# Loading a later pair's keys and values further along in the pair that is being worked on

## The chip, the cores and the metric

The kernel runs on one core of one Trainium2 chip. The metric is the device time of one execution in microseconds, as the median of several runs. The profile is that of one execution of its own.

## The reference, cut to what matters

Three layers follow one another on two batches of 768 positions.

```python
# 1: attention for 2 x 8 heads of 64, masked to pairs whose sign patterns under proj agree
mask = q_bucket[:, :, :, None] == k_bucket[:, :, None, :]
scores = np.where(mask, scale * np.matmul(q, k.transpose(0, 1, 3, 2)), -1e9)
attn = softmax(scores)
x = np.matmul(attn, v)            # heads side by side: 2 x 768 x 512
# 2: a mixing over positions of rank 32, then a two-layer perceptron 512 -> 2048 -> 512
u = x + (x.T @ U @ V).T
x = u + np.maximum(u @ w_ch1, 0.0) @ w_ch2
# 3: four gated causal attention experts, two of them kept at each position
```

The change touches only the loads of `q`, `k` and `v` of the first layer.

## The kernel before, in words

**Pairs and tiles.** The first layer works on two heads at a time, which the kernel calls a pair: four pairs for each batch, numbered here 0 to 7 in their order. A pair has 12 tiles of 128 queries each (`a1_head`, two heads of six). For a tile TensorE makes the scores (L606, L611), VectorE moves them to SBUF with their row minimum (L617), ScalarE takes the exponential (L526, or L575) and a float16 copy (L528), GpSimd or VectorE the remainder that the copy lost (L534). A transposing DMA turns the two halves (L628, `PT<-HL`; in batch 0 some of the buffers are parts of tiles called `more_W` and `more_hT`), and TensorE multiplies by the values (L538 to L540). In batch 0 every second tile keeps float32 and is turned on TensorE in place of the DMA (L581, L590); in batch 1 every tile is turned by the DMA. In batch 0 there are five buffers for each of the scores, the halves and the turned halves, in batch 1 three.

**What a pair does for later pairs.** At the start of pair i, `ahead` first calls `a1_prep` for pair i+1: ScalarE, VectorE and GpSimd make float16 halves of its queries (L403, L404) and keys (L408 on ScalarE, L409 and L414 on GpSimd), three transposing DMAs turn them (AQ L407, AK L412, KT L418), copies go to BQ and BK (L419, L421), and `a1_values` scales and splits the values (L454 on GpSimd, L455 on ScalarE, L456 on GpSimd). Six tiles later `signs` makes the sign patterns, and four small DMAs carry them (L446, L447). Then `a1_load` sets up the loads of pair i+2: six DMAs of 192 KB, one for each head of `q`, `k` and `v`. The buffers `qn`, `kn` and `vn` exist once, so a load must wait until the preparation of the pair before has read them. Every result of a load is needed by the preparation of its pair, which stands in the program at the start of pair i+1.

**What sets the order.** All these DMAs, and the loads of the perceptron's weights (L278, 32 units of 512 KB, three quarters of them within batch 0), are issued by SyncE in one queue (SP). `later(n, fn)` holds a step back until `tick()` has been called n times; `tick()` comes once for each tile. A scheduler of the language then lays the instructions out on the engines by their place in the program and by when it believes them ready, so that an engine with nothing due takes a later step early. On the chip each engine runs its own list in order.

**The other work.** The perceptron's weights are prepared on VectorE, ScalarE and GpSimd during batch 0 (`w64_unit`, L189 to L195 and L281 to L283). From the second half of pair 4 on, the perceptron's matmuls (L734, L754) are interleaved with the tiles, and after the first layer with the third.

Of the kernel before, what the change touches and what calls it, by code (L numbers as in the profile page):

```python
# [22 lines left out]
def kernel(  # L23
# [49 lines left out]
    XP = (0, 40)  # L73
    XV = True
    LUV = 4
    PLAG = (0,150)
    VLAG = 150
    PJ = nc.vector
# [266 lines left out]
    def later(n, fn):  # L345
        pending.append([n, fn])
# [10 lines left out]
    def sooner(n, fn):  # L357
        tc.cur_priority -= n
        fn()
        tc.cur_priority += n  # L360
# [7 lines left out]
    def a1_load(b, p, spread=True):  # L368
        h0 = 2 * p
        qn = sp.tile([P, 2 * NT, D], F32, tag="qn", name=f"qn_{b}_{p}")  # L370
        kn = sp.tile([P, 2 * NT, D], F32, tag="kn", name=f"kn_{b}_{p}")
        vn = sp.tile([P, 2 * NT, D], F32, tag="vn", name=f"vn_{b}_{p}")
        jt = [slice(NT * j, NT * (j + 1)) for j in range(2)]
        todo = []
        for j in range(2):
            todo.append((qn[:, jt[j], :], q[b, h0 + j].rearrange("(t p) d -> p t d", t=NT)))
            todo.append((kn[:, jt[j], :], k[b, h0 + j].rearrange("(p t) d -> p t d", t=NT)))
        for j in range(2):
            todo.append((vn[:, jt[j], :], v[b, h0 + j].rearrange("(p t) d -> p t d", t=NT)))
        nats[b, p] = (qn, kn, vn)  # L380
        todo = [lambda d=d, s_=s_: nc.sync.dma_start(d, s_) for d, s_ in todo]
        if spread:
            for i, fn in enumerate(todo):
                later(1 + i, fn)
        return todo

    preps = {}
# [71 lines left out]
    def a1_first(b, p):  # L459
        n = f"{b}_{p}"  # L460
        todo = a1_load(b, p, False)
        qn, kn, vn = nats.pop((b, p))
        QN = sp.tile([P, 2 * NT, P], FH, tag="QN", name=f"QN_{n}")
# [72 lines left out]
    def pv(o, PT, nk, vh, vl):  # L536
        for t in range(nk):
            nc.tensor.matmul(o, PT[:, t, :], vh(t), start=(t == 0), stop=False)  # L538
            nc.tensor.matmul(o, PT[:, t, :], vl(t), start=False, stop=False)  # L539
            nc.tensor.matmul(o, PT[:, nk + t, :], vh(t), start=False, stop=(t == nk - 1))  # L540
# [54 lines left out]
    def a1_head(b, p, j, xn):  # L595
# [7 lines left out]
        for t in range(NT):  # L603
# [17 lines left out]
            if mode[0] == "F":  # L621
# [6 lines left out]
            nc.sync.dma_start_transpose(out=PT, in_=HL.rearrange("p a s -> p (a s)"))  # L628
            sooner(-PLAG[b], lambda: pv(
                po[:, t, :], PT, NT,  # L630
# [59 lines left out]
    def a1_stream():  # L690
        pairs = [(b, p) for b in range(B) for p in range(NP)]
        for i, (b, p) in enumerate(pairs):
            if p == 0:
                if b == 1:
                    more_buffers(False)
            def ahead(i=i):
                if i + 1 < len(pairs):
                    a1_prep(*pairs[i + 1], SIGN_LAG)
                    if i + 2 < len(pairs):
                        a1_load(*pairs[i + 2])  # L700
                    else:
                        later(SIGN_LAG + 1, moe2_weights)

            if i == 0:
                later(2, ahead)
                later(LUV, load_uv)
            else:
                ahead()
            xn = sp.tile([P, NT, P], F32, tag="xn", bufs=XNB, name=f"xn_{b}_{p}")
            for j in range(2):  # L710
                for c in a1_head(b, p, j, xn):
                    tick()
                    yield c
            later(LAGX, lambda b=b, p=p, xn=xn: sooner(XP[p == NP - 1], lambda: x_stage_a(b, p, xn)))
# [362 lines left out]
    for fn in a1_load(0, 1, False):  # L1077
        fn()
# [126 lines left out]
```

## Time and profile before

| what | value |
|---|---|
| median of 3 runs | 636.65 us (636.04 to 637.46) |
| the profiled execution | 635.59 us, its span 633.8 us |
| TensorE matmul busy | 579.1 us (91%) |
| VectorE busy | 422.7 us (67%) |
| ScalarE busy | 348.5 us (55%) |
| GpSimd busy | 232.1 us (37%) |

A busy share is an average over the whole execution. The first layer takes the first 360 us and does not have the same limit all along; the views below cut it into stretches. The page draws the span in 40 slices of 15.8 us. The granted clock of TensorE is given as a share of full speed: 1.00 is 2.4 GHz and 0.50 is 1.2 GHz.

### The profile page before, as it was taken

The page shows a single profiled execution, that of the slowest core. Times are in us where ns is not written, and L with a number is a line of the kernel's source. Part 1 is how long each engine was busy: PE and PEld are TensorE (multiplying, and loading weights), DVE is VectorE, ACT ScalarE, POOL GpSimd, SP SyncE. Part 2 cuts the span into 40 slices and gives each one's busy share as a digit, 9 for nine tenths or more (in the row PEclk, how much of TensorE's full clock was granted, in tenths as well). Part 3 has the DMA queues.
Part 4 walks back from the last instruction along what each step waited for, and adds up shares of the span by engine and source line. Part 5 has one row for each costly group of instructions (what it writes and reads, how often), then busy time and mean ns, then how long its engine had stood idle before and what let it go on. Part 6 is the DMA issues. An engine that isn't in the chain of part 4 may idle for free.

```text
span 633.8 us, 16209 instructions
## 1 busy us (share of the span) xinstructions
PE 579.1 (91%) x6498; PEld 477.0 (75%) x6498; DVE 422.7 (67%) x1029; ACT 348.5 (55%) x744; POOL 232.1 (37%) x218
## 2 busy tenths in 40 slices
PE   5698888978798799989999999999999999998995
PEld 3376866757577589875888898878887888997963
DVE  6989696988877863674876555583784435465295
ACT  4769485775786652673776543462453413344273
POOL 4738777686897662231432101020040000002021
PEclk9679797889889999999999999999999999999998
DMA  8799999999989999597587602242263102016064
GB/s 234 140 218 215 243 211 244 227 228 269 219 182 251 231 178 172 101 200 114 108 130 121 101 20 50 38 84 72 46 114 67 34 15 39 27 35 109 23 107 109
DMA packets 228029, 84.36 MB, mean 133 GB/s; under 512 B 207057, under 2 KB 223473, under 8 KB 227953
## 3 DMA queue, kind: packets, MB, share of 16 engines
q1 hardware_dynamic: 227952, 83.32, 65.4%
q8 instruction: 51, 0.84, 0.6%
q14 instruction: 26, 0.20, 0.1%
HBM read 29.11 MB, written 3.15 MB: 51 GB/s over the span
## 4 chain that ended last, share of the span: by engine, by line
PE 59%; DMA 14%; DVE 7%; POOL 7%; ACT 6%; issue 5%; SPq 1%; POOLq 0%; DVEq 0%; ACTq 0%
PE px L754 18%; PE ph L734 12%; DMA PT<-HL 8%; PE po L590 3%; POOL HL L534 3%; PE pq L805 3%; PE s L908 2%; PE pk L805 2%; PE pz L1040 2%; PE pv L837 2%; ACT HL L528 2%; DVE P L617 2%; ACT P L526 2%; DMA more_hT<-more_W 2%; DMA more_hT<-HL 2%
## 5 line engine op out<-in xcount | busy, mean ns | idle before, releaser
L534 POOL TENSOR_TENSOR HL<-P,HL 128x768 f16<-128x768 f32 (+5 forms) x62 | 88.7, 1432 | 323.2 <-DVE HL L530 148.7
L734 PE MATMUL ph<-U,W 128*128 128x256 f16 (+1 forms) x1344 | 145.1, 258 | 1.7 <-DVE hT L736 1.1
L754 PE MATMUL px<-hT,W 128*128 128x256 f16 (+1 forms) x1344 | 146.1, 258 | 0.1
L734 PEld LDWEIGHTS <-W 128*128 128x128 f16 x1344 | 114.2, 98 | 17.1 <-issue 2.4
L754 PEld LDWEIGHTS <-W 128*128 128x128 f16 x1344 | 115.0, 98 | 14.3 <-issue 2.0
L526 ACT ACTIVATE P<-P,m 128x768 f32<-128x768 f32 (+5 forms) x109 | 88.7, 814 | 56.0 <-DVE P L916 28.7
L617 DVE TENSOR_SCALAR_CACHE_REDUCE P<-sc 128x768 f32<-128x768 f32 x76 | 71.9, 950 | 12.8 <-PE sc L611 8.4
L736 DVE SCALAR_TENSOR_TENSOR hT<-ph,hT 128x256 f16<-128x256 f32 (+1 forms) x112 | 42.6, 382 | 45.6 <-ACT hT L735 44.9
L528 ACT ACTIVATE HL<-P 128x768 f16<-128x768 f32 (+5 forms) x80 | 60.5, 758 | 17.6 <-DMA PT<-HL 14.8
L735 ACT ACTIVATE hT<-ph 128x256 f16<-128x256 f32 (+1 forms) x112 | 38.7, 347 | 51.3 <-PE ph L734 47.8
L538 PEld LDWEIGHTS <-PT 128*128 128x128 f16 x516 | 47.8, 99 | 23.8 <-DMA PT<-HL 20.1
L606 PE MATMUL sc<-AK,AQ 128*128 128x512 f16 x192 | 50.0, 341 | 9.3 <-DVE P L617 6.5
L538 PE MATMUL po<-V,PT 128*128 128x64 f16 x372 | 45.7, 195 | 11.5 <-DMA PT<-HL 10.6
L611 PE MATMUL sc<-BK,BQ 88*128 88x512 f16 x192 | 49.9, 340 | 0.0
L539 PEld LDWEIGHTS <-PT 128*128 128x128 f16 x516 | 47.5, 99 | 1.5 <-issue 0.2
L540 PEld LDWEIGHTS <-PT 128*128 128x128 f16 x516 | 47.4, 99 | 0.4
L540 PE MATMUL po<-V,PT 128*128 128x64 f16 x372 | 45.7, 195 | 0.0
L539 PE MATMUL po<-V,PT 128*128 128x64 f16 x372 | 45.2, 195 | 0.0
L534 DVE TENSOR_TENSOR HL<-P,HL 128x768 f16<-128x768 f32 (+5 forms) x42 | 32.3, 769 | 15.4 <-ACT HL L528 14.8
L916 DVE TENSOR_SCALAR_CACHE_REDUCE P<-s 128x128 f32<-128x128 f32 (+5 forms) x48 | 29.5, 618 | 10.9 <-PE s L913 10.6
L606 PEld LDWEIGHTS <-AQ 128*128 128x128 f16 x192 | 18.0, 105 | 17.8 <-issue 13.2
L611 PEld LDWEIGHTS <-BQ 88*128 88x128 f16 x192 | 19.5, 102 | 13.9 <-issue 2.1
(240 smaller groups left out, 1186.7 us busy)
## 6 DMA issues: line engine op xcount, KB each, us to landing
w<-in_moe_w_ch_dram SPq DMA_DIRECT2D x16, 512.0 KB
wx<-in_moe_w_ch_dram SPq DMA_DIRECT2D x16, 512.0 KB
qn<-in_q_dram SPq DMA_DIRECT2D x16, 192.0 KB
kn<-in_k_dram SPq DMA_DIRECT2D x16, 192.0 KB
vn<-in_v_dram SPq DMA_DIRECT2D x16, 192.0 KB
out_dram<-o SPq DMA_DIRECT2D x12, 256.0 KB
PT<-HL SPq DMA_TRANSPOSE x101
BQ<-AQ SPq DMA_DIRECT2D x7, 192.0 KB
```

Source lines behind the costliest of these rows:

```text
L526: nc.scalar.activation(P32, P32, AF.Exp, bias=m, scale=-1.0, accum_out=ssum)
L528: nc.scalar.activation(HL[:, 0], P32, AF.Copy)
L534: eng.tensor_tensor(HL[:, 1], P32, HL[:, 0], op=ALU.subtract)
L538: nc.tensor.matmul(o, PT[:, t, :], vh(t), start=(t == 0), stop=False)
L539: nc.tensor.matmul(o, PT[:, t, :], vl(t), start=False, stop=False)
L540: nc.tensor.matmul(o, PT[:, nk + t, :], vh(t), start=False, stop=(t == nk - 1))
L606: nc.tensor.matmul(ps[:, c0 : c0 + cn], aq[:, t, :], ak[:, c0 : c0 + cn], start=True, stop=False,)
L611: nc.tensor.matmul(ps[:, c0 : c0 + cn], bq[:, t, :], bk[:, c0 : c0 + cn], start=False, stop=True,)
L617: nc.vector.tensor_scalar(P32, ps[:, 0:S], CLIP, None, op0=ALU.min, op1=ALU.min, accum_out=m)
L734: nc.tensor.matmul(ph, w, u, start=(i == 0), stop=(i == len(ops) - 1))
L736: nc.vector.scalar_tensor_tensor(hT[1][:, ft, :], ph, 0.0, hT[0][:, ft, :], op0=ALU.max, op1=ALU.subtract)
L754: nc.tensor.matmul(po, w, u, start=(i == 0), stop=(i == len(ops) - 1))
```

## The change

The loads of pair i+2, which were issued after tiles 1 to 6 of pair i in the order q0, k0, q1, k1, v0, v1, are issued after tile 1 (q0), tile 3 (q1), tile 5 (k0), tile 6 (k1), tile 8 (v0) and tile 9 (v1). The queries keep their tiles. The first head's keys move by three tiles, the second head's by two, and the values by three. In pair 0 all of this counts from its third tile on, since `ahead` is called there two tiles late. Pairs 0 and 1 are loaded at the start without a delay, before and after.

```diff
+    LOADS = (1,3,5,6,8,9)
...
         if spread:
-            for i, fn in enumerate(todo):
-                later(1 + i, fn)
+            for i, n in zip((0, 2, 1, 3, 4, 5), LOADS):
+                later(n, todo[i])
         return todo
```

## Rows read from the trace of the kernel before

**Rows 1.** The page: the span, and the granted clock in 40 slices.
```profile
span 633.8 us, 16209 instructions
...
PEclk9679797889889999999999999999999999999998
```

**Rows 2.** Stretches: busy us (instructions) of PE, PEld, DVE, ACT, POOL; clock; DMA.
```profile
30.00:212.00 182.00, 155.99 (x1624) 124.59 (x1623) 149.23 (x288) 129.26 (x241) 133.16 (x115) 0.89 1.06 228
220.00:260.00 40.00, 40.00 (x459) 34.98 (x456) 21.73 (x42) 15.02 (x29) 15.45 (x14) 1.00 0.91 167
64.00:66.00 2.00, 0.55 (x3) 0.31 (x3) 2.00 (x4) 1.13 (x3) 1.84 (x3) 1.00 1.05 201
66.00:73.00 7.00, 6.60 (x60) 6.54 (x61) 2.59 (x8) 2.17 (x5) 5.42 (x5) 0.53 1.08 237
```

**Rows 3.** Timeline of SP, in pairs 0 to 2: start, duration, line, DMA.
```profile
21.70 0.35 SPq L381 DMA_DIRECT2D vn<-in_v_dram  x1
...
65.02 0.59 SPq L381 DMA_DIRECT2D kn<-in_k_dram  x1
65.73 1.74 SPq L628 DMA_TRANSPOSE PT<-HL  x1
...
68.81 0.53 SPq L381 DMA_DIRECT2D kn<-in_k_dram  x1
69.52 3.58 SPq L628 DMA_TRANSPOSE more_hT<-HL  x1
...
73.77 0.43 SPq L381 DMA_DIRECT2D vn<-in_v_dram  x1
...
77.97 0.51 SPq L381 DMA_DIRECT2D vn<-in_v_dram  x1
...
82.41 1.47 SPq L628 DMA_TRANSPOSE more_hT<-more_W  x1
...
90.27 3.42 SPq L412 DMA_TRANSPOSE AK<-KN  x1
93.75 1.28 SPq L418 DMA_TRANSPOSE KT<-KL  x1
...
124.77 2.44 SPq L412 DMA_TRANSPOSE AK<-KN  x1
```

**Rows 4.** Timeline of POOL; in brackets its idle time before and what ended it.
```profile
75.33 0.83 POOL L409 TENSOR_SCALAR KN<-KN 128x768 f16<-128x768 f16 x1 [3.74 <-ACT KN L408]
76.12 2.50 POOL L414 TENSOR_TENSOR KL<-kn,KN 128x384 f16<-128x384 f32 x2
...
80.74 1.64 POOL L534 TENSOR_TENSOR more_W<-more_W,more_W 128x768 f16<-128x768 f32 x1 [0.18 <-ACT more_W L528]
85.25 1.65 POOL L534 TENSOR_TENSOR more_W<-P,more_W 128x768 f16<-128x768 f32 x1 [2.87 <-ACT more_W L528]
...
113.27 0.86 POOL L409 TENSOR_SCALAR KN<-KN 128x768 f16<-128x768 f16 x1 [3.79 <-ACT KN L408]
```

**Rows 5.** The chain that ended last, in order of time: start, duration, what.
```profile
82.41 6.45 DMA more_hT<-more_W
...
97.87 4.96 DMA PT<-HL
...
163.22 6.10 DMA more_hT<-HL
...
189.30 4.14 DMA vn<-in_v_dram
```

**Rows 6.** Who waited for whom from 30 to 212: total us, times, longest.
```profile
POOL KN L409 <- ACT KN L408: 11.5, 4, 3.8
...
PE po L538 <- DMA PT<-HL: 6.3, 6, 2.7
...
PE po L538 <- DMA more_hT<-HL: 4.5, 2, 3.0
...
PE po L538 <- DMA more_hT<-more_W: 3.4, 2, 2.6
```

## The prediction

> **What bounds the kernel now.** I begin with the page. Its clock line has low digits from the second slice to the twelfth (16 to 190 us) and full ones from there almost to the end [rows 1]; so I cut near there. In the table of stretches TensorE is busy all 40.00 of 40 us from 220 to 260, at full clock: from there on TensorE's own work sets the pace, and a DMA that moves inside it is covered [rows 2]. From 30 to 212 us no engine is full: of 182 us TensorE has 155.99 busy, VectorE 149.23, GpSimd 133.16 and ScalarE 129.26, at a mean granted clock of 0.89, while the DMA engines show a share of 1.06 and 228 GB/s [rows 2]. This is the stretch of pairs 0 to 4, and it is the only place where the change can be worth anything.
>
> Inside it the pace comes in waves, one for each pair. At the restart of a pair TensorE runs dry (0.55 busy of 2 us from 64 to 66, with VectorE at 2.00 of 2.00), then it has work again, but for the next 7 us the clock is at its lower level (0.53 on average, 0.50 is 1.2 GHz), and now VectorE and ScalarE idle (2.59 and 2.17 of 7) [rows 2]. One such wave costs 7 x (1 - 0.53) = 3.3 us of TensorE. The chain of waits says what the restart waits for: transposed halves that land 5 to 6 us after SP has issued them [rows 5]. All TensorE's waits for such landings from 30 to 212 us are 6.3 + 4.5 + 3.4 = 14.2 us [rows 6]. That is the pot out of which the change could pay.
>
> **What the change does to SP.** In pair 1 the old order had k0 at 65.02 and k1 at 68.81, each right ahead of a transpose (65.73 and 69.52), v0 at 73.77, and v1 at 77.97 behind the four sign DMAs [rows 3]. In the new order k0 takes about v0's place, k1, at tile 6 behind the signs, about v1's place, and v0 and v1 stand ahead of the transposes of tiles 8 and 10. Nothing is added: the four loads cost SP 0.59 + 0.53 + 0.43 + 0.51 = 2.06 us of issue for a pair, before and after. On the DMA engines one load is 192 KB, which at the 237 GB/s of the stretch from 66 to 73 is an estimate of 0.83 us [rows 2].
>
> **Step 1, the transposes after a restart.** Each k load leaves the way of a transpose: at most 0.59 + 0.83 = 1.4 us. From 66 to 73 TensorE is busy 6.60 of 7 us at half clock, so an earlier landing has nothing to shorten there, and I count nothing for pairs 1 to 3. In pair 4 the restart's landing stands in the chain with 6.10 us, against 4.96 where no load stood ahead [rows 5]. The difference, 1.14, is the most that a load taken away may give; I take half, -0.6. Bounds 0 and -1.1.
>
> **Step 2, the transposes late in a pair.** v0 and v1 now precede transposes that had none. The one at 82.41 is on the chain with 6.45 us until it landed [rows 5], so a load ahead of it can count in full: 0.43 + 0.83 = 1.3 us, in three pairs 3.8. But a tile takes some 3 us and v0 has most of that to drain. I take 0.4 for a pair, +1.2. Bounds 0 and +3.8.
>
> **Step 3, the keys' preparation.** GpSimd waits 11.5 us in four pairs for ScalarE's copy of the keys, 3.74 of it at 75.33, and then spends 0.83 + 2.50 = 3.33 us on them [rows 4, 6]. This lies within the wave's idle part, and the next remainder, at 80.74, was released by ScalarE only 0.18 us before it began, so GpSimd's own wait delayed nothing. With the keys 77.97 - 68.81 = 9.2 us later, the work falls to about 84.5. There GpSimd has a hole of 2.87 us ahead of 85.25 [rows 4], which takes nearly all of the 3.33; the overhang is 0.46 us. In return ScalarE, which has to serve the waiting tiles first after a restart, is rid of one copy of about 0.83 us (taken from GpSimd's row on the same 128 x 768 elements). I take half, 0.4 us, for four pairs: -1.6. Bounds -3.3 (all of it) and +1.8 (the overhang in four pairs).
>
> **Step 4, the last value load of pair 6.** It is on the chain itself, at 189.30 with 4.14 us, stuck behind sign DMAs [rows 5]. Three tiles later it is no longer what these tiles meet. The chain will find another way, mostly a transpose's landing, so I take a third, -1.4. Bounds 0 and -4.1.
>
> **The sum** is -0.6 + 1.2 - 1.6 - 1.4 = -2.4 us. Made against the profiled execution it is 635.59 (its span 633.8, and 1.8 around it) - 2.4 = 633.2. The median of the runs is 1.06 above that execution, so the forecast is 634.25, rounded to 634.2: 0.4% faster. A measurement of this kernel can tell about 0.2%, which is 1.3 us.
>
> **The rivals.**
>
> *The keys fall into the full half of a pair.* If the load lands only a few us later than I assume, its 3.33 us of GpSimd come after 85.25, in the part where VectorE and GpSimd have no hole left and the remainders feed the transposes of the next restart. For it: the hole at 82.4 is the only one seen there; late in a wave VectorE is full. Against it: GpSimd is busy only 133.16 of 182 us. It decides when the keys' first GpSimd step begins after 85 in pair 1. At about 0.9 us for a pair, between the overhang of 0.46 and the full 3.33, four pairs give +3.6: 640.3 us. Slower.
>
> *The keys come too late for their own transposes.* AK and KT stand in SP's queue ahead of the next pair's first transposes, and SP waits at them with everything behind it. In pair 1 GpSimd was done with AK's input at 76.2, and SP got to AK at 90.27: 14 us of slack, 5 after the move. In pair 2 it was 114.13 against 124.77 [rows 3, 4]: 10.6 us of slack, 1.4 after the move of 9.2. The time is bounded from below by nothing, and from above by a wait of the 9.2 us itself in a pair; I put 1 us in two pairs, +2.0: 638.6 us. The Trainium skill, in "DMA: Bandwidth & Descriptors", section "Rules for kernel authors", asks to issue a DMA early and to wait for it late; the change does the reverse, and by that rule it could only lose. The rows agree so far as slack shrinks from 10.6 to 1.4 us, and do not show it used up.
>
> *It is hidden either way.* The queries, which are the first thing needed, keep their tiles, the later loads may be covered by their slack, and what one transpose wins another loses: 636.6 us. To this belongs that the change may do less than it says: the scheduler sent a value load at 21.70, well ahead of the queries of its pair, since nothing else was due [rows 3], and may send the later loads early too. Against that, in pair 1 the order of SP is that of the program.
>
> **How the numbers follow.** The pot is small and no step dominates, and each shift also shifts what the scheduler packs around it; so the chances lie close. My forecast has 0.42, "hidden" 0.25, the full half of a pair 0.20, the late keys 0.13. That gives faster 0.42, same 0.25, slower 0.33. The forecast's own range is 630.0 to 635.4: the low end is the sum, one half-clock wave less (-3.3) and a part of the free bounds of steps 3 and 4. The range over all cases needs the slower rivals, both well over 0.1, so it runs from 630.0 to 641.0, which leaves about 1 in 10 on each side outside.
>
> **What the profile after would show.** SP's list in pair 1 should have one load between each two of its transposes, k1 behind the four sign DMAs, and v1 ahead of the last transpose but none of these loads within the first 5 us after the restart except q0. GpSimd's wait for the keys should shrink from 11.5 us, and its keys' steps should stand some 9 us later. The chain should no longer hold a value load. Step 2 is right if landings late in a pair grow by less than 1 us. The forecast is wrong if the table of stretches shows a new low clock in the middle of a pair, if GpSimd is fuller and VectorE emptier before the restarts, if SP waits at AK or KT for GpSimd, or if TensorE becomes full from 30 us at a later time than now. Since the stretch after 220 is TensorE's alone, whatever is won must show as an earlier start of that full stretch.

## The result and the profile after

The changed kernel takes 641.49 us (median of four runs, 639.4 to 645.47) against 636.35 for the kernel before (four runs, 628.08 to 637.46; three of them are those shown ahead of the prediction): ratio 1.0115, 95% interval 1.0068 to 1.0162, so slower. Here and below the ratio is estimated over the single runs, without runs of a kernel more than 1.5% above its fastest, and is not the quotient of the two medians, which is 1.0081 here. The forecast was 634.2 us with a range of 630.0 to 641.0; the sign was wrong and the time lies just above the range. The profiled execution took 642.95 us, its span is 7.4 us longer than before.

All line numbers past the new one are higher by 2 in the changed kernel: L381 is now L383, L628 L630, L538 L540, L409 L411.

The page of the changed kernel, span and granted clock:

```profile
span 641.2 us, 16217 instructions
...
PEclk9778887998787989999999999999999999999998
```

Against [rows 1], the lower digits reach to the fifteenth slice; from the sixteenth on the two lines are alike. The table of stretches of the changed kernel (columns as in [rows 2]):

```profile
30.00:212.00 182.00, 156.12 (x1538) 122.79 (x1538) 146.00 (x281) 123.86 (x228) 129.66 (x114) 0.84 1.04 221
220.00:260.00 40.00, 38.12 (x413) 32.90 (x410) 19.68 (x36) 15.46 (x29) 13.39 (x12) 0.96 0.82 162
...
76.00:84.00 8.00, 7.68 (x59) 5.28 (x60) 6.71 (x14) 4.92 (x8) 5.51 (x6) 0.57 1.00 261
...
193.00:200.00 7.00, 6.08 (x53) 4.33 (x53) 6.26 (x13) 4.51 (x8) 3.52 (x4) 0.52 1.00 223
```

From 30 to 212 us TensorE is as busy as before (156.12 for 155.99) at a lower clock (0.84 for 0.89), so it gets less done. A new low clock stands in the middle of pair 1 (0.57 from 76 to 84) and late in pair 4 (0.52 from 193 to 200), which the prediction had named as a sign against it. From 220 to 260 TensorE is no longer full (38.12 of 40 us for 40.00), so the stretch that TensorE paces by itself begins later.

Roughly where the time is lost shows in VectorE's closing step of each head (`xn`, two in each pair). Its timeline before, for the sixth to the tenth head and the last:

```profile
133.31 0.55 DVE L639 TENSOR_TENSOR xn<-po,r 128x384 f32<-128x384 f32 x1
150.65 0.56 DVE L639 TENSOR_TENSOR xn<-po,r 128x384 f32<-128x384 f32 x1 [0.16 <-PE po L590]
173.15 0.56 DVE L639 TENSOR_TENSOR xn<-po,r 128x384 f32<-128x384 f32 x1 [3.09 <-PE po L590]
190.98 0.55 DVE L639 TENSOR_TENSOR xn<-po,r 128x384 f32<-128x384 f32 x1
217.34 0.55 DVE L639 TENSOR_TENSOR xn<-po,r 128x384 f32<-128x384 f32 x1
...
363.34 0.55 DVE L639 TENSOR_TENSOR xn<-po,r 128x384 f32<-128x384 f32 x1
```

and the same heads in the changed kernel:

```profile
133.83 0.56 DVE L641 TENSOR_TENSOR xn<-po,r 128x384 f32<-128x384 f32 x1 [0.54 <-PE po L592]
158.02 0.55 DVE L641 TENSOR_TENSOR xn<-po,r 128x384 f32<-128x384 f32 x1
179.06 0.56 DVE L641 TENSOR_TENSOR xn<-po,r 128x384 f32<-128x384 f32 x1 [2.79 <-PE po L592]
202.80 0.56 DVE L641 TENSOR_TENSOR xn<-po,r 128x384 f32<-128x384 f32 x1 [0.39 <-PE po L542]
224.18 0.55 DVE L641 TENSOR_TENSOR xn<-po,r 128x384 f32<-128x384 f32 x1
...
371.35 0.55 DVE L641 TENSOR_TENSOR xn<-po,r 128x384 f32<-128x384 f32 x1
```

At the end of pair 2 the kernels are level (+0.5 us). The changed one is 7.4 behind halfway through pair 3 and 5.9 after it, 11.8 halfway through pair 4 and 6.8 after it, 8.0 at the end of the layer. Pair 1's new low clock thus cost nothing that lasted. By these rows most of the lag stands after pair 3, and pair 4 adds 0.9 to it. They are a rough measure: the place of `xn` in VectorE's list can move, and in pair 4 other matmuls are interleaved.

What pair 3 lost begins at its restart, where TensorE waits for a transpose. Before, in SP's and TensorE's timelines:

```profile
133.25 2.19 SPq L628 DMA_TRANSPOSE more_hT<-HL  x1
```

```profile
138.31 0.24 PE L538 MATMUL po<-V,more_hT 128*128 128x64 f16 x1 [2.95 <-DMA more_hT<-HL]
```

and in the changed kernel:

```profile
135.90 1.14 SPq L423 DMA_DIRECT2D BK<-KT  x2
137.12 1.49 SPq L630 DMA_TRANSPOSE more_hT<-HL  x1
```

```profile
141.71 0.24 PE L540 MATMUL po<-V,more_hT 128*128 128x64 f16 x1 [4.26 <-DMA more_hT<-HL]
```

GpSimd's first step for pair 4's keys begins at 123.19, against 113.27 [rows 4], and AK goes out at 128.88, against 124.77 [rows 3]. SP then waits 2.1 us for KT to land before it copies it to BK, and the restart's transpose stands behind that copy. So the restart comes 3.4 us later, behind keys that are turned late.

SP's timeline in pair 1, which the prediction had drawn in advance:

```profile
73.30 0.44 SPq L383 DMA_DIRECT2D kn<-in_k_dram  x1
...
77.80 0.51 SPq L383 DMA_DIRECT2D kn<-in_k_dram  x1
78.50 1.31 SPq L630 DMA_TRANSPOSE PT<-HL  x1
79.85 0.58 SPq L383 DMA_DIRECT2D vn<-in_v_dram  x1
...
84.10 0.58 SPq L383 DMA_DIRECT2D vn<-in_v_dram  x1
```

and GpSimd's, with the waits of that stretch (the changed kernel, 30 to 212 us):

```profile
81.86 0.83 POOL L411 TENSOR_SCALAR KN<-KN 128x768 f16<-128x768 f16 x1 [1.25 <-ACT KN L410]
```

```profile
ACT QN L405 <- DMA qn<-in_q_dram: 7.8, 2, 4.6
...
DVE w_x L191 <- DMA w<-in_moe_w_ch_dram: 7.5, 3, 4.4
...
POOL KN L411 <- ACT KN L410: 3.2, 2, 1.9
...
ACT KN L410 <- DMA kn<-in_k_dram: 2.7, 2, 1.7
```

The loads stand where the program put them, GpSimd's wait for the keys falls from 11.5 [rows 6] to 3.2 us, and its step moves only from 75.33 [rows 4] to 81.86, not to 84.5. ScalarE, the keys' first reader, now waits 2.7 us for their loads; GpSimd waits 0.4 us for values. Grown far more are ScalarE's waits for queries (0.4 us before) and VectorE's for these weights (1.4 before), neither of which the change touches by its text.

TensorE's largest wait that has no counterpart before is in pair 4. The changed kernel's SP, VectorE and TensorE there, in three timelines:

```profile
185.34 0.92 SPq L383 DMA_DIRECT2D vn<-in_v_dram  x2
186.30 0.43 SPq L280 DMA_DIRECT2D wx<-in_moe_w_ch_dram  x1
```

```profile
192.32 0.69 DVE L191 TENSOR_SCALAR w_x<-wx 128x512 uint32<-128x512 uint32 x1 [3.22 <-DMA wx<-in_moe_w_ch_dram]
192.92 0.95 DVE L212 SCALAR_TENSOR_TENSOR U<-up,U 128x768 f16<-128x768 f32 x1
```

```profile
193.92 1.01 PE L736 MATMUL ph<-U,W 128*128 128x256 f16 x4 [3.73 <-DVE U L212]
```

VectorE waits 3.22 us for a weight load; `U` stands behind that step in its list, TensorE waits 3.73 us for `U`, and the low clock of 193 to 200 follows. Before, VectorE waited for a weight load too (2.45 us), but with `U` already made, as its timeline shows:

```profile
185.44 0.96 DVE L210 SCALAR_TENSOR_TENSOR U<-up,U 128x768 f16<-128x768 f32 x1 [0.98 <-ACT U L209]
...
194.84 0.69 DVE L189 TENSOR_SCALAR w_x<-wx 128x512 uint32<-128x512 uint32 x1 [2.45 <-DMA wx<-in_moe_w_ch_dram]
```

So the order in VectorE's list changed, though nothing in the change names VectorE.

### The profile page after: what moved, and what is told of

It is laid out like the page before. It is cut to its first block, busy times and chain, and to the rows that moved or that the text cites. A ratio compares the mean times of both kernels' runs of the same rounds, so it can differ in the third digit from the quotient of the medians.

```text
span 641.2 us, 16217 instructions
## 1 busy us (share of the span) xinstructions
PE 586.7 (91%) x6498; PEld 481.1 (75%) x6498; DVE 421.8 (66%) x1029; ACT 348.8 (54%) x744; POOL 230.5 (36%) x218
## 4 chain that ended last, share of the span: by engine, by line
PE 59%; DMA 17%; POOL 8%; DVE 6%; ACT 4%; issue 4%; SPq 1%; DVEq 0%; POOLq 0%; ACTq 0%
PE px L756 18%; PE ph L736 14%; DMA PT<-HL 9%; POOL HL L536 3%; PE po L592 3%; DMA w<-in_moe_w_ch_dram 3%; PE pq L807 3%; PE s L910 2%; PE pk L807 2%; PE pv L839 2%; PE pz L1042 2%; PE sc L608 2%; PE sc L613 2%; DMA KT<-KL 2%; POOL W L285 1%
## 5 line engine op out<-in xcount | busy, mean ns | idle before, releaser
L756 PE MATMUL px<-hT,W 128*128 128x256 f16 (+1 forms) x1344 | 147.6, 258 | 0.0
L540 PEld LDWEIGHTS <-PT 128*128 128x128 f16 x516 | 48.9, 101 | 23.8 <-DMA PT<-HL 17.2
L608 PE MATMUL sc<-AK,AQ 128*128 128x512 f16 x192 | 52.8, 358 | 8.2 <-DVE P L619 6.0
L540 PE MATMUL po<-V,PT 128*128 128x64 f16 x372 | 47.6, 199 | 9.1 <-DMA PT<-HL 6.8
L613 PE MATMUL sc<-BK,BQ 88*128 88x512 f16 x192 | 53.0, 358 | 0.0
L541 PEld LDWEIGHTS <-PT 128*128 128x128 f16 x516 | 48.7, 101 | 1.6 <-issue 0.2
L542 PEld LDWEIGHTS <-PT 128*128 128x128 f16 x516 | 48.7, 101 | 0.3
L542 PE MATMUL po<-V,PT 128*128 128x64 f16 x372 | 47.4, 198 | 0.0
L541 PE MATMUL po<-V,PT 128*128 128x64 f16 x372 | 47.2, 198 | 0.0
L918 DVE TENSOR_SCALAR_CACHE_REDUCE P<-s 128x128 f32<-128x128 f32 (+5 forms) x48 | 29.5, 618 | 10.9 <-PE s L915 10.6
```

The costliest lines, as they stand in the source:

```text
L608: nc.tensor.matmul(ps[:, c0 : c0 + cn], aq[:, t, :], ak[:, c0 : c0 + cn], start=True, stop=False,)
L613: nc.tensor.matmul(ps[:, c0 : c0 + cn], bq[:, t, :], bk[:, c0 : c0 + cn], start=False, stop=True,)
L756: nc.tensor.matmul(po, w, u, start=(i == 0), stop=(i == len(ops) - 1))
```

## The experiments

Three theories were on record. **A**: the late value loads cost (in front of transposes, and heaped with weight loads behind pair 4's sign DMAs). **B**: the late keys cost, since their preparation moves into the full half of a pair. **C**: any shift lets the scheduler lay the lists of all engines out anew, the lists of before happen to run well, and new ones run worse. Ratios are to the kernel before on the same chip, with 95% intervals.

### One part of the change at a time

All these edit the one loop; where TILES stands, each kernel has one of the lists below, as (load, tile), with loads 0 to 5 for q0, k0, q1, k1, v0, v1.

```diff
-            for i, fn in enumerate(todo):
-                later(1 + i, fn)
+            for i, n in TILES:
+                later(n, todo[i])
...
# values late:  (0,1) (1,2) (2,3) (3,4) (4,8) (5,9)
# keys late:    (0,1) (2,3) (1,5) (4,5) (3,6) (5,6)
# order only:   (0,1) (2,2) (1,3) (3,4) (4,5) (5,6)
# one later:    (0,2) (1,3) (2,4) (3,5) (4,6) (5,7)
# v1 later:     (0,1) (1,2) (2,3) (3,4) (4,5) (5,7)
# pair 6 old:   the new tiles, but the old ones in pair 6
# pair 6 new:   the old tiles, but the new ones in pair 6
```

Values late:

> Only the values are late (tiles 8 and 9); queries and keys stay at tiles 1 to 4 as before. Theory A (the late value loads cost the time: ahead of the transposes at a pair's end, and in one heap with weight loads behind the sign DMAs of pair 4): 640 to 644 us, +4 to +7 on before. Theory B (the keys' preparation, moved into the full half of a pair, costs it): within 1.5 us of before. Theory C (any shift re-packs the schedule, and this one came out badly): anywhere within 5 us of before.

638.67 us, 1.0064 (1.0033 to 1.0095).

Keys late:

> Only the keys are late (tiles 5 and 6, the second query load at tile 3); the values stay at tiles 5 and 6. Theory A: within 1.5 us of before. Theory B: 640 to 644 us. Theory C: anywhere within 5 us of before.

636.90 us, 1.0034 (1.0008 to 1.0060).

The first head's keys after the second head's queries, and no more:

> The six loads at tiles 1 to 6 as before, only the second head's queries ahead of the first head's keys (tiles 2 and 3 trade places). Nothing is late, so theories A and B both say within 1.5 us of before. Theory C: it may move as far as the whole change did, 3 us or more either way; how far it moves is the measure of what a re-packed schedule alone does.

639.42 us, 1.0070 (1.0040 to 1.0100).

Pair 6 old:

> The changed kernel, but pair 6 (loaded while pair 4 is worked on) with the loads of before. In the trace of the changed kernel 4.7 of the loss arises in the second half of pair 4, where both value loads and two weight loads are issued in one heap ahead of a transpose. Theory A: that part is gone, 636.5 to 638.5 us, and no half-clock stretch near 193 us. Theory B: the keys of pairs 2 to 5 still cost, 640 us or more. Theory C: no definite number.

638.51 us, 1.0061 (1.0034 to 1.0088).

Pair 6 new:

> The kernel before, with only pair 6 (loaded while pair 4 is worked on) on the new tiles; everything up to pair 4 is laid out as before. Theory A (the heap of value and weight loads behind pair 4's sign DMAs): +3 to +5 us on before, and a stall of TensorE near 190 us. Theory C (a re-packed schedule comes out badly, whatever is moved): no definite place; a loss as large would have to show with harmless shifts too.

636.56 us, 1.0062 (1.0034 to 1.0090).

All six loads one tile later:

> All six loads one tile later (2 to 7 in place of 1 to 6), in the old order. The distance to their use shrinks by one tile of some eight, so theories A and B give under 1 us (A at most a little for the last value load, at tile 7). Theory C: +2 to +5 us, as the mere swap of two loads gave.

642.65 us, 1.0131 (1.0086 to 1.0177): more than the whole change.

Only the last load one tile later:

> The smallest change that there is: only the last value load one tile later (7 in place of 6). Theories A and B: under 0.5 us. Theory C: the lists of the engines differ in hundreds of lines, so +1 to +4 us is possible. If it stays within 0.2% of before, theory C needs more than a shift as such.

637.06 us, 1.0042 (1.0013 to 1.0071).

The new tiles, with the values' loads issued from ScalarE's queue:

```diff
-        todo = [lambda d=d, s_=s_: nc.sync.dma_start(d, s_) for d, s_ in todo]
+        todo = [lambda d=d, s_=s_, e=e: e.dma_start(d, s_)
+                for (d, s_), e in zip(todo, [nc.sync] * 4 + [nc.scalar if spread else nc.sync] * 2)]
```

> The new tiles, but the late value loads are issued by ScalarE's queue, so that they stand neither in SP's list ahead of the transposes nor behind the sign DMAs; their bytes run on the same DMA engines. Theory A in its SP part: 636 to 639 us, 3 us or more better than the changed kernel. If it is the bytes and not SP's list: 640 us or more. Theory C: between 636 and 642 us, without a reason to prefer.

645.43 us, 1.0181 (1.0142 to 1.0220). Freeing SP's list won nothing, which speaks against A's queue part; it does not settle it, since the lists were laid out anew here too and GpSimd waited 7.5 us for the values (0.4 in the changed kernel). The Trainium skill says in "DMA: Bandwidth & Descriptors", section "Issuing engines are not separate DMA queues", that issuing from several engines only saves the time to issue; this run agrees in so far as nothing was won.

What follows: the parts do not rank by how late they make anything. Two neighbouring loads exchanged cost 0.70%, one load by one tile 0.42%. That fits C; A and B have no account of it. For pair 6 alone the times do fit A (+3 to +5 us for pair 6 new, 636.5 to 638.5 for pair 6 old, the second at its edge), but the stall that A wanted near 190 us is not in the trace of pair 6 new: from 163 to 215 TensorE's longest wait there is 1.6 us.

### Controls that move no load of queries, keys or values

```diff
-    LUV = 4
+    LUV = 5
# or
-    SIGN_LAG = 6
+    SIGN_LAG = 7
```

The step that loads and prepares U and V (of the mixing) a tile later, with the old tiles:

> A control that leaves every load of queries, keys and values at its old tile: only the one load of U and V, 2 tiles' worth of small data in pair 0, is issued one tile later (LUV 5 for 4). It re-lays part of the lists of all engines. Theory C (any shift re-packs lists that came out well): slower by 0.2 to 1.3%, 634.5 to 641.5 us against a before of some 633.2. Theories A and B (late values, late keys): within 0.2% of before, since nothing they speak of moves.

643.81 us, 1.0135 (1.0092 to 1.0178).

The sign patterns a tile later, with the old tiles:

> A second control with the old tiles of all loads: only the sign patterns of the next pair are made one tile later (SIGN_LAG 7 for 6), so that the second value load stands ahead of the sign DMAs. It re-lays more of the lists than the first control. Theory C: slower by 0.2 to 1.3%, 634.5 to 641.5 us. Theory A: not slower, rather faster by up to 0.3%, since the value load no longer stands behind the sign DMAs. Theory B: within 0.2%.

642.53 us, 1.0145 (1.0114 to 1.0177).

The same two edits on the changed kernel:

> The changed kernel, its loads at the new tiles, with the one load of U and V a tile later. Theory C: the extra time of the changed kernel depends on how the lists come out, so this one may stand anywhere from 0.2 to 1.5% above before, and more likely off the changed kernel's 1.15% than on it. Theories A and B: 0.9 to 1.4% above before, as the changed kernel.

643.59 us, 1.0168 (1.0131 to 1.0205).

> The changed kernel, its loads at the new tiles, with the sign patterns a tile later, so that the second head's keys stand ahead of the sign DMAs. Theory C: anywhere from 0.2 to 1.5% above before. Theory A: 0.9 to 1.4% above, since the value loads stay where they are. Theory B (late keys): better than the changed kernel by 0.2 to 0.5%, since the keys of the second head land sooner.

645.18 us, 1.0191 (1.0146 to 1.0235).

Both controls lose as much as the change, with every load of `q`, `k` and `v` at its old tile. C's ranges were even too short, for all four of these, for one tile later and for ScalarE's queue. What the controls move is later by itself too, but in the first two the waits show no engine that waits for the loads of U and V or for the sign DMAs. The new tiles stood, with their own lists, at 1.0115, 1.0168 and 1.0191; the old ones, laid out anew, at 1.0135 and 1.0145. So a cost of the late tiles by themselves, beyond that of being laid out anew, is not seen here, nor ruled out at the size of the gaps between these numbers.

### The lists held fixed

A list is pinned by building the kernel, reading each engine's list, and building it again with an edge that keeps the order of issue between each two neighbours. Only then are single instructions moved: a load goes ahead of the transpose that it precedes in the other kernel.

```diff
+        for names in (lists or dict()).values():
...
+            for a, c in zip(names, names[1:]):
+                tc.add_manual_dep(made[c], a, dep, reason="list")
...
+    for k, r in goes:
+        sp.remove(load[k])
+        sp.insert(sp.index(turn[r]), load[k])
```

Lists of before, keys and values at the new places:

> Every engine keeps the list of the kernel before, instruction by instruction; only in SP's list the loads of keys and values stand ahead of those transposes ahead of which they stand in the changed kernel. Theory C (the re-laid lists cost, not the loads): within 0.3% of before, 631 to 636 us. Theories A and B together (the loads' new places cost): 0.8 to 1.4% slower, 638 to 643 us. The forecast's own four steps, which spoke of the loads alone, would make it 2.4 us faster, 0.4%.

662.88 us, 1.0427 (1.0396 to 1.0458).

Lists of before, keys alone:

> The lists of before, with the loads of keys alone at the new places. Theory C: within 0.3% of before. Theory B (late keys): 0.4 to 1.2% slower. Theory A: within 0.2%.

650.05 us, 1.0241 (1.0204 to 1.0278).

Lists of before, values alone:

> The lists of before, with the loads of values alone at the new places. Theory C: within 0.3% of before. Theory A (late values): 0.4 to 1.2% slower. Theory B: within 0.2%.

651.33 us, 1.0258 (1.0222 to 1.0293).

None of the theories had expected so much, and C as first put, that the loads' places cost nothing, fell here. ScalarE's timeline in pair 1 of the kernel before, then SP's and ScalarE's with the keys moved:

```profile
73.66 0.84 ACT L403 ACTIVATE QN<-qn 128x768 f16<-128x768 f32 x1 [0.41 <-DMA qn<-in_q_dram]
74.41 0.83 ACT L408 ACTIVATE KN<-kn 128x768 f16<-128x768 f32 x1
```

```profile
81.03 0.90 SPq L381 DMA_DIRECT2D kn<-in_k_dram  x2
```

```profile
84.86 0.84 ACT L408 ACTIVATE KN<-kn 128x768 f16<-128x768 f32 x1 [7.99 <-DMA kn<-in_k_dram]
85.61 0.79 ACT L209 ACTIVATE U<-up 128x768 f16<-128x768 f32 x1
...
86.82 0.92 ACT L526 ACTIVATE more_W<-more_W,m 128x768 f32<-128x768 f32 x1
```

The copy of the keys stands right behind that of the queries in ScalarE's list. Moved away, the load lands 84.86 - 81.03 = 3.8 us after its issue, and ScalarE stands for 7.99 us with `U` and the next tile's exponential behind it. By the same 3.8 us the second keys' load of before (68.81, [rows 3]) landed at an estimated 72.6, and its reader began at 74.41: 1.8 us of slack. The waits from 30 to 212 us show it in three pairs each, first of the kernel with the keys moved, then of the one with the values moved:

```profile
ACT KN L408 <- DMA kn<-in_k_dram: 24.8, 3, 8.5
```

```profile
POOL vn L454 <- DMA vn<-in_v_dram: 21.6, 2, 11.7
...
POOL more_hT L454 <- DMA vn<-in_v_dram: 5.4, 1, 5.4
```

(In one of the pairs the step's result goes to a part of `more_hT`.) Beside 24.8 us of waits for the keys stand 15.3 us of time (0.0241 x 635.43), beside 27.0 for the values 16.4. One limit: in these kernels the keys are issued at 81.03, where the changed kernel issues the last at 77.80, so the place is some 3 us worse than in it.

The lists of before, for pairs 2 to 6 with the readers moved along (each line with the numbers of its instructions that move: copies, remainders, the keys' transposes and the copies behind them):

```diff
+READERS = {408: range(1, 6), 409: range(1, 6), 414: range(2, 12), 412: range(1, 6), 418: range(1, 6), 421: range(2, 12), 454: range(2, 7), 455: range(2, 7), 456: range(2, 7)}
...
+    def moves(k):
+        if isinstance(k[0], int):
+            return k[2] in MOVED and 2 <= 4 * k[0] + k[1] < 7
+        return k[1] in READERS and k[2] in READERS[k[1]]
```

> Every engine keeps the list of the kernel before, except for the loads of keys and values of pairs 2 to 6 and for what reads them: ScalarE's and GpSimd's preparation of the keys and values, the transposes of the keys' halves and the copies behind them, which all stand ahead of the same tile's work as in the changed kernel. If the rest of the lists makes the change's loss: within 0.3% of before, since the stalls of the readers are gone. If the later preparation of keys and values costs by itself: 0.8 to 1.5% slower, as the changed kernel or a little more.

659.92 us, 1.0388 (1.0342 to 1.0434). Its waits from 30 to 212 us:

```profile
PE sg L436 <- DMA AK<-KN: 9.9, 3, 4.0
...
ACT KN L408 <- DMA kn<-in_k_dram: 2.3, 1, 2.3
```

The copy's wait has shrunk to 2.3 us, and the next reader has one: the matmuls of the sign patterns stand in TensorE's list where the keys used to be turned by then. GpSimd still waits for values here, 9.6 us in two waits. Lateness is handed down the chain of readers as far as the lists are held.

Now the lists of the changed kernel with the loads taken back:

> The reverse: every engine keeps the list of the changed kernel, and in SP's list the loads of keys and values stand where they stand in the kernel before (all but one, the second head's keys of pair 7, which keep their new place). Theory C: as slow as the changed kernel, 0.8 to 1.5% above before. Theories A and B: back to before, within 0.3%.

653.86 us, 1.0295 (1.0258 to 1.0331). This run does not answer the question: pair 6's second keys load went out late, and ScalarE waited 13.05 us for it at 189.34. The next one leaves the loads of pairs 6 and 7 as in the changed kernel:

> Every engine keeps the list of the changed kernel; in SP's list the loads of keys and values of pairs 2 to 5 stand where they stand in the kernel before, those of pairs 6 and 7 stay at the new places. If the late loads themselves still cost something in the changed kernel (transposes held up by them, readers that wait): better than the changed kernel by 0.4 to 1.2%, so within 0.7% of before. If the rest of the lists makes the loss: 0.9 to 1.4% slower than before, as the changed kernel.

642.70 us, 1.0112 (1.0067 to 1.0158): as the changed kernel. At pair 3's restart TensorE waits 4.42 us for the transpose, as in the changed kernel. VectorE's and TensorE's timelines in pair 4 show the changed kernel's stall again:

```profile
190.67 0.69 DVE L189 TENSOR_SCALAR w_x<-wx 128x512 uint32<-128x512 uint32 x1 [3.46 <-DMA wx<-in_moe_w_ch_dram]
191.28 0.95 DVE L210 SCALAR_TENSOR_TENSOR U<-up,U 128x768 f16<-128x768 f32 x1
```

```profile
192.28 1.01 PE L734 MATMUL ph<-U,W 128*128 128x256 f16 x4 [3.98 <-DVE U L210]
```

With the lists of the changed kernel, early loads give no measurable time back in pairs 2 to 5, though the two intervals leave room for some half a per cent. These lists keep the keys' preparation late (GpSimd's first step for pair 4's keys is at 120.69), so the run does not tell the late preparation from the rest of the lists. Pair 6's value loads, which precede `wx` in that stall, were not taken back here. They were in the kernel with pair 6 old. Its SP and VectorE in pair 4, in two timelines:

```profile
185.05 0.52 SPq L382 DMA_DIRECT2D vn<-in_v_dram  x1
185.61 0.54 SPq L279 DMA_DIRECT2D wx<-in_moe_w_ch_dram  x1
```

```profile
190.94 0.69 DVE L190 TENSOR_SCALAR w_x<-wx 128x512 uint32<-128x512 uint32 x1
191.54 0.95 DVE L211 SCALAR_TENSOR_TENSOR U<-up,U 128x768 f16<-128x768 f32 x1
```

Here `U` stands behind the weights in VectorE's list too, but one value load less is ahead of `wx`. VectorE, which comes to that step 1.8 us later than in the changed kernel (190.94 against 192.32 - 3.22), finds it landed, and TensorE waits 0.6 us for `U`. So list and load seem to make this stall together: with `U` first (before) a wait for `wx` does not hold TensorE, with `wx` in time (pair 6 old) the list does not. The lists of pair 6 old are its own, so this is argued and not shown. The kernel with pair 6 old is at 1.0061, the changed one at 1.0115; their intervals overlap, so pair 6's share of about 0.5% is likely and not shown.

No kernel tried beats the one before.

## Why the prediction was wrong

**What bounds the kernel**: right. 6.8 of the 8.0 us of lag at the end of the layer are there by the end of pair 4, the stretch that TensorE paces begins later, and low clock goes with the loss.

**Step 1** (the transposes after a restart, -0.6): right as far as it goes. In pair 4 the restart's landing in the chain of waits took 4.43 us in place of 6.10 [rows 5], 1.67 less where the step allowed 1.14, so the load alone does not account for it. It did not last: some 20 us later the chain holds a landing of 7.86.

```profile
165.93 4.43 DMA PT<-HL
...
187.40 7.86 DMA PT<-HL
```

**Step 2** (the transposes late in a pair, +1.2, bounds 0 to +3.8) is one of the two steps that failed. It priced the value loads by the transposes behind them and forgot who reads the values. With the lists held they cost 16.4 us, through GpSimd's `vn` step, four times the bound. The run with ScalarE's queue, slower still, speaks against the queue as the matter. In the changed kernel itself, with lists laid out anew, GpSimd waits only 0.4 us for values.

**Step 3** (the keys' preparation, -1.6, bounds -3.3 to +1.8) failed in the same way and by more. It looked for room where the work would fall, and took the copy off ScalarE's hands. But the copy has a place in ScalarE's list, and with the lists held it waited there: 15.3 us lost, at a place some 3 us later than in the changed kernel. In the changed kernel itself that wait is 2.7 us. The slack that I worked out among the rivals, 14 and 10.6 us, was that of a late reader, AK in SP's list. The first reader, the copy at 74.41, had 1.8. The row at 74.41 would have told.

**Step 4** (the last value load of pair 6, -1.4): the load is off the chain, as foreseen, and a transpose's landing of 7.86 us stands in its place, longer than the 4.14 [rows 5] it replaced. The two value loads now precede weight loads that VectorE waits for.

**The sum** lacked the largest term, and this is the step that failed for the time measured. It was made as though every other instruction kept its neighbours; in the text the scheduler appears only as a reason for close chances. In fact the scheduler laid all lists out anew. That took back most of what late loads cost with lists held (27.1 us, 0.0427 x 635.43, at places some 3 us worse), and left new lists that run slower than those of before. Laid out anew with no load of `q`, `k` or `v` moved, they cost 8.6 us (0.0135 x 633.7) and 9.2; the change's own 1.15% is 7.3 us. It is of that size, and it stays when pairs 2 to 5 have their early loads back (1.0112).

**The rivals**: "the keys fall into the full half of a pair" (640.3) came nearest in time, by luck: its sign, a first GpSimd step after 85 in pair 1, did not come (81.86), GpSimd's wait shrank, and the keys alone cost 0.34%. "Too late for their own transposes" (638.6) happened once in the changed kernel, at pair 3's restart, where SP waited 2.1 us for KT with the restart's transpose behind it; but the run with early loads and the same lists waits there too (4.42 us in TensorE), so the list carries it. With the lists of before held it showed at the sign matmuls. The rule beside it, in the Trainium skill's "DMA: Bandwidth & Descriptors", section "Rules for kernel authors", to issue a transfer early and wait late, agrees with the runs that held the lists (2.41 and 2.58% slower). "Hidden" (636.6) is out by the interval.

**Still open**: how the 1.15% divides between bad luck in the lists and the later preparation as such. The intervals do not separate old tiles laid out anew (1.0135, 1.0145) from the new tiles (1.0115 to 1.0191). Why every layout tried ran slower than that of before is not settled either; the twelve other kernels in which the scheduler laid the lists out itself were 0.34 to 1.91% slower, and no rule for a good layout was found.

## What to carry to other kernels

The slack of a load is the time to its first reader in that engine's list, since everything behind the reader waits too; work it out there, one reader after the other, and not at the end of the chain. Where a scheduler lays out the lists, a one-line shift is a new draw for all engines: before crediting or blaming the shift, run a control that moves something unrelated by as much, here worth 1.35 and 1.45%. To learn what a shift does by itself, hold the lists and move only it.

## What the runs showed that was not expected

Low clock followed a stall late in a pair as it does a restart: after TensorE's 3.73 us of waiting at 193.92, the granted clock was 0.52 from 193 to 200, near its level of 1.2 GHz, at 6.08 busy of 7 us. By an estimate from these figures that stretch costs 6.08 x (1 - 0.52) = 2.9 us of TensorE on top of the wait. In the runs that the ratios use, the kernel before spread from 627.14 to 640.04 us over all sessions, 2.1%, so that half a per cent is near the edge of what the intervals here can tell.
